# Scores of a threshold attention in tiles of 64 rows by 64 columns, two heads by two halves of 128 queries

## The chip, the cores and the metric

The kernel runs on one core of one Trainium2 chip. Its time is the device time of that core in microseconds (us). The core has five engines that matter here: TensorE (PE in the profile, with its weight loads shown apart as PEld), VectorE (DVE), ScalarE (ACT), GpSimd (POOL) and the queue that issues the transfers (SP).

## The reference

Everything is in float32. For each of 8 batches and 8 heads there are 576 queries, keys and values of 64 features.

```python
scores = (1 / 8) * q @ k.T                       # 576 x 576 for each head
thresh = max(scores, axis=-1) - tau
scores = where(scores >= thresh, scores, -1e9)
attn = exp(scores - max(scores))
attn = attn / (sum(attn) + 1e-9)
o = attn @ v                                     # (8, 8, 576, 64) -> x: (8, 576, 512)
xn = (x - mean(x)) / sqrt(var(x) + 1e-6) * g_ln
out = x + relu(xn @ w_ch1) @ w_ch2               # 512 -> 2048 -> 512
```

## The kernel before, in words

**Steps.** The work is a row of 72 steps, nine (SLOTS) for each batch. In a batch, steps 0 to 3 take one pair of heads each (hp) and the first 256 queries of both heads; steps 5 to 8 take the same pairs and the next 256 queries. Step 4 (s == HP) takes the last 64 queries of all eight heads. So each step has 512 rows of scores against 576 keys, laid out as four blocks of 128 rows.

**Scores.** `scores` (L376) writes into two rooms of PSUM, `sc[0]` and `sc[1]`, one for each head of the pair, of three banks each. Head h lies on partitions 64h to 64h+63 of q and k, so the two heads use the two halves of PE's rows. A block of 128 queries by 576 keys begins at column 128 of its room and the next follows it, so the blocks cross the banks' bounds; `span` (L369) cuts them there into pieces of 384, 192, 320 and 256 columns. The pieces of the two heads are issued in turn. In an ordinary step a product takes 128 queries as its stationary operand (a tile of 64 rows by 128 columns of PE); in step 4 two pairs of heads lie beside each other in each block, so a product takes 64 queries (64 by 64) and `i` goes over two of them. Each product appears in the trace as two instructions of PE.

**After the scores.** `exponentials` (L397) takes the rows' maxima on DVE (neg, L407), the thresholds on POOL (thr, L411) and the exponentials on ACT (e, L419). `weights` (L423) masks, sums (DVE, L426) and divides. The result is turned: in the first batch by products with diagonals on PE (`turn_weights`, tp and tr), later by DVE and a trip through DRAM (`turn_blocks` and `fetch`, which give the tiles em and er).

**Values.** `values_of` multiplies v with the turned weights. The first 512 keys (em, L574) go over all 128 rows of PE and 64 columns, a tile of 128 by 64; the last 64 keys (er, L584) are on 64 rows, a tile of 64 by 64. Except in the first six steps, where both are done at once and er too uses 128 rows (pv in the trace), the er products are put off to the start of the step after next, in the call `run(n, -3)` that stands just ahead of `scores(b, s)` in the main loop (L1007, L1008). The sums lie behind the scores in the same rooms of PSUM (`pv_behind`).

**FFN.** Between the quarters of each step `second_part` (L950) issues pieces of the FFN of groups of 288 tokens: the first product (p) and the second one (seg), which is done as seven products of quarters with sums of quarters of the weights. Every such product goes through `product` (L96), which splits its 128 output rows into two tiles of 128 by 64 that stream the same moving operand.

**Order.** The schedule is written by hand: each engine carries out its instructions in the order in which this program issues them. The queues `later_calls` (by step and quarter), `aside`, `stores` and `drops` say when put-off work is issued. The number of FFN pieces in each quarter follows from counts in the program (ROOM, ends, ready), and not from times.

Of the kernel before, what the change touches and what calls it, by code (L numbers as in the profile page):

```python
# [18 lines left out]
def kernel(  # L19
# [36 lines left out]
    HP = H // 2  # L56
# [307 lines left out]
    sc = [ps_sc.tile([128, 3 * 512], F32, name=f"sc{i}") for i in range(2)]  # L364
# [4 lines left out]
    def span(at, n):  # L369

        while n:
            m = min(n, 512 - at % 512)
            yield at, m
            at, n = at + m, n - m

    def scores(b, s):  # L376


        hp, half = (s, 0) if s < HP else (s - HP - 1, 1)

        pieces = []
        for h in range(2):
            t = 0
            for j in range(2):
                first = FREE + j * S
                for at, n in span(first, S):
                    pieces.append((t, h, j, at, n, at - first))
                    t += n
        for t, h, j, at, n, o in sorted(pieces):
            r = slice(64 * h, 64 * h + 64)  # L390
            for i in range(2 if s == HP else 1):
                qT, kT, ql = turned[b * HP + (2 * j + i if s == HP else hp)]
                nc.tensor.matmul(  # L393
                    sc[h][64 * i : 64 * i + 64 if s == HP else 128, at : at + n],
                    lhsT=ql[r] if s == HP else qT[r, half, j * 128 : (j + 1) * 128],
                    rhs=kT[r, o : o + n], start=True, stop=True,
                )  # L397

# [600 lines left out]
    for n in range(NS):  # L999
        b, s = divmod(n, SLOTS)  # L1000
# [5 lines left out]

        run(n, -3)  # L1007
        scores(b, s)  # L1008
        run(n, -2)
        run(n, -1)  # L1010
# [104 lines left out]
```

## Time and profile before

| | |
|---|---|
| Time, median of 3 runs | 1398.31 us (1396.4 to 1398.57) |
| Span of the profiled execution | 1398.0 us |
| PE matmul busy | 1332.8 us, 95% |
| PE weight load busy | 1011.1 us, 72% |
| DVE, ACT, POOL busy | 928.2, 464.2, 607.1 us |
| Scores of ordinary steps, L393, tile 64*128 | 1024 matmuls, 152.7 us busy |
| Scores of step 4, L393, tile 64*64 | 256 matmuls, median 402 ns |
| Products with v over the first 512 keys, L574, tile 128*64 | 2368 matmuls, 129.5 us busy |
| er products behind, L584, tile 64*64 | 480 of 295 ns and 112 of 230 ns |

Busy times of PE add instructions that run side by side in different tiles only once, and the mean of one is its own length, ends modelled; so a row's count times its mean is more than its busy time. A form such as 64*128 64x384 means a tile of 64 rows and 128 columns, and a moving operand of 64 partitions by 384 elements. In a row of the waits the columns are: who waited, for whom, total us, times, longest us.

### The profile page before, as it was taken

What the parts mean: (1) busy time and instruction counts of PE and PEld (TensorE: products, weight loads), DVE (VectorE), ACT (ScalarE), POOL (GpSimd) and SP (SyncE); (2) the same over time, 40 slices, a digit from 0 to 9 for tenths busy, and PEclk for the clock granted to TensorE, in tenths of its full rate; (3) what the DMA queues carried; (4) which work ended last, traced back from release to release, by engine and by line L of the source; (5) the groups of instructions that cost most, each with busy time, mean ns of one, the idle gap of its engine ahead of it and who ended that gap; (6) DMA issues with size and microseconds to landing.
All of it is one profiled execution on the core that took longest, in us unless ns stands there. A gap on an engine that the chain in (4) does not pass through costs nothing.

```text
span 1398.0 us, 38357 instructions
## 1 busy us (share of the span) xinstructions
PE 1332.8 (95%) x16336; PEld 1011.1 (72%) x16336; DVE 928.2 (66%) x1638; ACT 464.2 (33%) x1003; POOL 607.1 (43%) x807
## 2 busy tenths in 40 slices
PE   4788989999999999999999999999999999999996
PEld 3665655867768696877869687786968687686966
DVE  5898867676776767657776667657675767766211
ACT  3777613232332323232232322323232323323120
POOL 2344444544443544443444445353444444434313
PEclk9999999999999999999999999999999999999998
DMA  9722355446734476446754476445763476343211
GB/s 222 188 77 71 92 139 153 166 141 183 200 128 163 141 196 174 146 141 183 199 159 146 150 191 179 152 150 144 197 181 131 143 183 183 131 162 129 65 18 18
DMA packets 322011, 206.72 MB, mean 148 GB/s; under 512 B 247984, under 2 KB 279472, under 8 KB 313776
## 3 DMA queue, kind: packets, MB, share of 16 engines
q1 hardware_dynamic: 317072, 203.68, 50.2%
q8 instruction: 128, 2.10, 0.6%
q10 hardware_dynamic: 4736, 0.59, 0.4%
q14 instruction: 43, 0.35, 0.1%
q0 software_dynamic: 32, 0.00, 0.0%
HBM read 120.46 MB, written 83.76 MB: 146 GB/s over the span
## 4 chain that ended last, share of the span: by engine, by line
PE 83%; DVE 7%; ACT 2%; DMA 2%; issue 2%; POOL 1%; SPq 1%; POOLq 0%; DVEq 0%; ACTq 0%
PE p L101 34%; PE seg L101 27%; PE sc L393 10%; PE sc L574 8%; PE sc L584 2%; DVE e L426 2%; DVE neg L407 1%; DMA v_in<-in_v_dram 1%; SPq L116 1%; PE tp L101 1%; DMA et<-in_moe_w_ch_dram 1%; POOL q_in L341 1%; PE var L101 0%; PE mean L101 0%; POOL sum L626 0%
## 5 line engine op out<-in xcount | busy, mean ns | idle before, releaser
L101 PE MATMUL p<-xc,w 128*64 128x288 f32 x4096 | 518.1, 408 | 12.9 <-ACT hidden L779 5.5
L101 PEld LDWEIGHTS p<-xc,w 128*64 128x64 f32 x4096 | 287.5, 137 | 219.7 <-ACT hidden L779 16.1
L407 DVE TENSOR_REDUCE neg<-sc 128x2 f32<-128x1152 f32 x144 | 188.7, 1351 | 251.1 <-PE sc L393 251.1
L101 PE MATMUL seg<-hidden,w 128*64 128x144 f32 x3840 | 248.3, 287 | 3.8 <-DVE hidden L847 3.8
L101 PEld LDWEIGHTS seg<-hidden,w 128*64 128x64 f32 x3840 | 234.9, 137 | 14.6 <-issue 6.5
L411 POOL TENSOR_SCALAR thr<-neg,low_sb 128x2 f32<-128x2 f32 x144 | 42.5, 295 | 466.0 <-DVE neg L407 461.0
L442 POOL TENSOR_SCALAR e<-e,den 128x576 f32<-128x576 f32 x252 | 194.3, 785 | 114.5 <-DVE den L431 114.5
L426 DVE SCALAR_TENSOR_TENSOR e<-sc,thr,e 128x576 f32<-128x576 f32 x288 | 221.9, 809 | 16.5 <-POOL thr L411 14.6
L779 ACT ACTIVATE hidden<-p 128x288 f32<-128x288 f32 x256 | 106.6, 417 | 321.9 <-PE p L101 321.8
L419 ACT ACTIVATE e<-sc,neg 128x576 f32<-128x576 f32 x288 | 197.8, 754 | 8.2 <-DVE neg L407 8.2
L393 PE MATMUL sc<-kT,qT 64*128 64x384 f32 (+3 forms) x1024 | 152.7, 429 | 24.1 <-DVE e L426 14.0
L516 DVE STREAM_TRANSPOSE et<-e 128x1152 f32<-128x1152 f32 x112 | 153.2, 1374 | 18.2 <-POOL e L442 17.7
L393 PEld LDWEIGHTS sc<-kT,qT 64*128 64x128 f32 x1024 | 95.6, 192 | 65.3 <-DVE e L426 18.9
L574 PE MATMUL sc<-em,v_in 128*64 128x128 f32 (+1 forms) x2368 | 129.5, 263 | 0.0
L574 PEld LDWEIGHTS sc<-em,v_in 128*64 128x64 f32 x2368 | 122.9, 137 | 7.8
L101 PE MATMUL seg<-hidden,stage 128*64 128x144 f32 x1920 | 123.3, 286 | 0.0
L101 PEld LDWEIGHTS seg<-hidden,stage 128*64 128x64 f32 x1920 | 117.6, 137 | 2.5 <-issue 2.5
L597 ACT COPY x<-sc 128x128 f32<-128x128 f32 x120 | 31.8, 266 | 260.7 <-PE sc L393 193.5
L847 POOL TENSOR_TENSOR hidden<-hidden 128x576 f32<-128x576 f32 x60 | 84.8, 1429 | 47.8 <-ACT hidden L779 38.2
L862 ACT COPY part<-seg 128x288 f32<-128x288 f32 x75 | 30.3, 403 | 198.3 <-PE seg L101 194.2
L847 DVE TENSOR_TENSOR hidden<-hidden 128x576 f32<-128x576 f32 x60 | 49.2, 854 | 49.1 <-PE seg L101 39.1
L101 PE MATMUL seg<-hidden,e 128*64 128x144 f32 x960 | 65.3, 286 | 0.0
(152 smaller groups left out, 1112.9 us busy)
## 6 DMA issues: line engine op xcount, KB each, us to landing
scr<-et SPq DMA_DIRECT2D x63, 1152.0 KB, 5.0
em<-scr SPq DMA_DIRECT2D x63, 1024.0 KB, 5.7
out_dram<-ot SPq DMA_DIRECT2D x256, 36.0 KB, 3.6
q_in<-in_q_dram SPq DMA_DIRECT2D x124, 72.0 KB, 2.5
k_in<-in_k_dram SPq DMA_DIRECT2D x120, 72.0 KB, 2.8
er<-scr SPq DMA_DIRECT2D x126, 64.0 KB, 5.1
v_in<-in_v_dram SPq DMA_DIRECT2D x28, 256.0 KB, 5.5
w<-in_moe_w_ch_dram SPq DMA_DIRECT2D x10, 512.0 KB, 6.2
```

The lines of the kernel that those rows point to most:

```text
L101: nc.tensor.matmul(out[r], lhsT=lhsT[:, r], rhs=rhs, **flags)
L393: nc.tensor.matmul(sc[h][64 * i : 64 * i + 64 if s == HP else 128, at : at + n], lhsT=ql[r] if s == HP else qT[r, half, j * 128 : (j + 1) ...
L407: nc.vector.tensor_reduce(out=neg[:, i], in_=pairs[h], axis=AXL.X, op=ALU.max, negate=True,)
L411: nc.gpsimd.tensor_scalar(out=thr[:, i], in0=neg[:, i], scalar1=-1.0, scalar2=low_sb, op0=ALU.mult, op1=ALU.add,)
L419: nc.scalar.activation(es[:, i], blocks[i], func=AF.Exp, bias=neg[:, i : i + 1])
L426: nc.vector.scalar_tensor_tensor(out=es[:, i], in0=blocks[i], scalar=thr[:, i : i + 1], in1=es[:, i], op0=ALU.is_ge, op1=ALU.mult, accum_o ...
L442: nc.gpsimd.tensor_scalar(out=es[:, i], in0=es[:, i], scalar1=den[:, i : i + 1], scalar2=1.0, op0=ALU.mult, op1=ALU.mult,)
L516: nc.vector.transpose(et[:, :, 64 * h : 64 * h + 64].rearrange("p n (j c) -> p j n c", j=2), es[:, 2 * h : 2 * h + 2].rearrange("p j (n c) ...
L574: nc.tensor.matmul(dst[64 * h : 64 * h + 64], lhsT=vt[:, h, c, :], rhs=pick(em[:, 2 * j : 2 * j + 2, c], h), start=c == 0 and first, stop= ...
L597: nc.scalar.copy(x_of(2 * b + (s > HP))[:, s % (HP + 1), 128 * j : 128 * j + 128], pv[j])
L779: nc.scalar.activation(hidden[:, d], p1, func=AF.Relu)
L847: eng.tensor_tensor(out=out[at], in0=in0[at], in1=in1[at], op=op)
```

## The change

All scores are done in tiles of 64 rows by 64 columns. Where one product took 128 queries, two now take 64 each, written to the lower and upper half of the same 128 partitions. What each computes, the pieces, the streamed columns of kT and the order of the pieces stay as they were. The aim is that the scores use the tiling of PE that the er products with v just ahead of them use, and that four tiles (two heads by two halves) work at once.

```diff
         for t, h, j, at, n, o in sorted(pieces):
             r = slice(64 * h, 64 * h + 64)
-            for i in range(2 if s == HP else 1):
+            for i in range(2):
                 qT, kT, ql = turned[b * HP + (2 * j + i if s == HP else hp)]
                 nc.tensor.matmul(
-                    sc[h][64 * i : 64 * i + 64 if s == HP else 128, at : at + n],
-                    lhsT=ql[r] if s == HP else qT[r, half, j * 128 : (j + 1) * 128],
+                    sc[h][64 * i : 64 * i + 64, at : at + n],
+                    lhsT=ql[r] if s == HP else qT[r, half, j * 128 + 64 * i : j * 128 + 64 * i + 64],
                     rhs=kT[r, o : o + n], start=True, stop=True,
                 )
```

## The prediction

> **What bounds the kernel now.** I read three views in this order: the table of busy time by stretches of 100 us, to see where TensorE (PE) is the limit; the waits of the matmul queue outside the start-up; and the timeline of PE around two blocks of scores, because the kernel before already holds both forms side by side.
>
> ```profile
> 300.00:400.00 100.00, 99.33 (x1135) 72.83 (x1134) 74.30 (x135) 32.17 (x70) 46.09 (x62) 1.00 0.62 172
> ...
> 1100.00:1200.00 100.00, 99.33 (x1138) 72.84 (x1136) 71.10 (x129) 31.77 (x69) 49.13 (x65) 1.00 0.60 170
> ```
>
> The columns are the stretch, its length, then busy us and instructions of PE, weight load (PEld), VectorE (DVE), ScalarE (ACT) and GpSimd (POOL), the granted clock, DMA share and GB/s. From 300 to 1300 us every stretch shows PE busy 98.8 to 99.4 us of 100 at full clock, while DVE, ACT and POOL stay at or below 75 (PEld belongs to PE). Only the first 250 us or so and the last 80 are otherwise. Busy matmuls alone don't prove that PE is at its peak, so I also read what PE waits for from 150 to 1280 us:
>
> ```profile
> PE p L101 <- ACT part L862: 4.0, 7, 0.6
> PE seg L101 <- DVE hidden L847: 3.8, 6, 0.6
> PE p L101 <- ACT hidden L779: 1.8, 1, 1.8
> ```
>
> These are the three largest of nine. All nine come to 14 us, and none of them lies ahead of a score or in the er products. So PE in its written order is what sets the time there, and each tenth of a microsecond saved inside its stream moves the end, as long as the work behind it doesn't turn into a wait.
>
> Now the two blocks of scores, batch 4, some 18 us apart. In the rows: start, length, instructions in the run; after the operation's names comes the shape of the PE tile, rows*columns.
>
> ```profile
> 705.50 2.11 PE L101 MATMUL p<-xc,w 128*64 128x288 f32 x16
> 707.53 0.45 PE L584 MATMUL sc<-er,v_rest 64*64 64x128 f32 x8
> 707.91 2.21 PE L393 MATMUL sc<-kT,qT 64*128 64x384 f32 x16
> 710.05 6.04 PE L101 MATMUL p<-xc,w 128*64 128x288 f32 x48
> ...
> 723.25 3.08 PE L101 MATMUL p<-xc,w 128*64 128x288 f32 x24
> 726.26 0.45 PE L584 MATMUL sc<-er,v_rest 64*64 64x128 f32 x8
> 726.53 2.12 PE L393 MATMUL sc<-kT,q_last 64*64 64x384 f32 x32
> 728.58 4.10 PE L101 MATMUL p<-xc,w 128*64 128x288 f32 x32
> ```
>
> The first is an ordinary step: products of the FFN in tiles of 128*64, the er products in 64*64, the scores in 64*128, the FFN again in 128*64. The second is the step of the last queries (s == HP), whose scores are already in 64*64. Both compute the same number of scores over the same 1152 columns per tile. Ends are modelled, so I take starts only: er to FFN is 710.05 - 707.53 = 2.52 us in the first, 728.58 - 726.26 = 2.32 us in the second. The first loses 0.11 between er and the scores (0.38 against 0.27 from start to start) and 0.09 from the scores to the FFN (2.14 against 2.05).
>
> **What the Trainium skill says.** "TensorEngine Tiling (Array Packing)", Key Properties: "Changing tiling mode (not just tile) drains the TensorE". The trace agrees in kind: with the mode kept from er to scores, the scores start 0.11 us sooner. The same page, Available Configurations, gives four independent tiles for 64x64 and two for 64x128, so both forms can fill the whole array. The trace agrees: 32 instructions of 64*64 take no longer than 16 of 64*128. "TensorE: Matmul & The Clock Gate", LDWEIGHTS, says that the load's time goes with the number of weight columns; here a load takes 187 ns for 128 columns and 133 ns for 64, so the fall is less than half. The tiling page's Gotcha 1 forbids different row tiles to use one PSUM bank at once; the two heads (row tiles) write sc0 and sc1, and that stays.
>
> **The change part by part.** 72 calls of scores() are made, 8 of them in the s == HP form that isn't touched. In the other 64, each of 8 products (16 instructions) of 128 queries becomes two of 64, 16 products (32 instructions), over the same kT columns.
>
> 1. Entrance. Where the er products lie directly ahead, 64*64 is kept instead of switched. I went through all 72 blocks: from the eighth on (120.92 us) the er products always lie directly ahead, in 58 blocks of the changed form and 7 of the other. Start to start is 0.37 to 0.40 us in the 58 and 0.26 to 0.27 in the 7: 0.11 us saved for each.
>
> 2. Streaming. FFN products of 288 columns run x48 in 715.93 - 710.05 = 5.88 us, which is 245 ns for a pair of column tiles. A score tile streams 1152 columns twice, 2304/288 x 245 ns = 1.96 us. The 64*64 block takes 2.05 to the next start and the 64*128 block 2.13 to 2.15 in all 58. So four tiles do run side by side at the full rate, and what is left above streaming shrinks from 0.18 to 0.09: another 0.09 us saved. Why the exit is shorter, fewer weight columns to put in place or a cheaper switch, the trace doesn't say; I need only the sum.
>
> 3. Added instructions. 64 x 16 = 1024 matmuls and as many loads. In a block, PEld goes from 16 x 187 = 3.0 us to 32 x 133 = 4.3 us of load time, but on four tiles at once. The s == HP block carries precisely this count in 2.05 us, so I put it at nothing beyond item 2, hidden beneath the streaming of the other tiles. One thing differs from that block: its two column tiles of one head stream different kT, and the changed block's two stream the same kT. The FFN products do that too: product() at L101 sends one rhs to both column tiles, at the 245 ns a pair used above. Bound: nothing to, if the second tile had to wait for the first, 2 us.
>
> 4. What follows. No wait is added and the order of all other work is kept. The maxima (DVE neg L407) wait on the scores' end and come 0.2 us sooner against the step's start; POOL thr, q_in, DVE qT and once per batch the hidden sum at L847 hang on them, and PE's 0.6 us wait on L847 starts its chain at a score's end, so it moves along unshortened. The wait on ACT part L862 is PE to ACT to PE and keeps its size too. DVE at 63 to 74 of 100 us has room for a step that is about 1.2% shorter. The weights fetched for the values (em<-scr, 5.7 us to land) are asked for at quarter 0 and used at quarter 3 of a step of 17 to 20 us; PE never waits for them now.
>
> Sum: per block 2.52 - 2.32 = 0.20 us. From 246 us on, 52 blocks x 0.20 = 10.4 us, all on the path. The six blocks from 120.92 to 228.34 us lie where the chain of waits runs partly through DVE's and ACT's conversion of weights; of their maxima some three start off PE and the others off a busy DVE, so I count half: 0.6 us. The six changed blocks before 100 us come after 128*64 products (pv), so the entrance switch stays, and PE waits there for DVE anyway: 0 (bound 6 x 0.09 = 0.5). Total 11.0 us: 1398.3 - 11.0 = 1387.3 us.
>
> **Rivals.**
> A. Only the entrance is saved: the exit keeps its 2.14 us because it hangs on something that the s == HP block doesn't have. For it: that block is always followed by FFN products, never by seg. Against: 64*128 blocks leave at 2.14 whether p or seg follows. 58 x 0.11 = 6.4 us, giving 1391.9 us.
> B. The time is taken back by waits: PE reaches ACT's copies or the conversion sooner and stands. For it: start-up shows it. Against: nine kinds of wait at 14 us in all, with DVE at 70%. If less than half came through, 3 to 5 us faster, 1394; at the utmost nothing, 1398.
> C. Slower: shared kT, or the doubled loads, keep the four tiles from running together. If merely the added 16 loads of 133 ns were a tenth exposed, that is 0.2 us x 64 = 14 us, with the switch saved some 3 us slower, 1401; if the two column tiles ran one after the other, 64 x 2 = 128 us, 1526. For it: the exact form isn't in the trace. Against: items 2 and 3.
>
> **How the numbers follow.** Forecast 0.82, A 0.08, B 0.06 (half of it within 0.2%), C 0.04 (a quarter of it within). The range: the low end takes all 58 blocks at 0.20 and the early 0.5 (12.1 us, 1386.2) and below it the spread of the three times before (2.2 us), 1384.3; the high end is just short of A, 1391.5. Outside it is left A, B and C, 0.18. Faster by over 0.2% (2.8 us) 0.93, within it 0.04, slower 0.03.
>
> **What would show it.** Right: L393 in one form only, 64*64 x2304; er to scores 0.27 us and scores to the next product 2.05 us in all blocks after 120 us; PE still busy over 99% from 300 to 1300 us, and its waits at about 14 us. Wrong at item 1: 0.38 stays. Wrong at item 2 or 3: over 2.1 us from scores to the next product, or gaps inside the block. Wrong at item 4: new PE waits on ACT hidden L779, DVE xc L649 or DVE hidden L847, with blocks as short as forecast. Wrong altogether if the span doesn't fall by about 58 times what a block falls.

## The result and the profile after

The changed kernel takes 1388.68 us (median of 4 runs, 1387.83 to 1388.95), the one before, measured beside it, 1397.68 us (4 runs, 1396.4 to 1398.57). The ratio is 0.9935 with a 95% interval of 0.9918 to 0.9952: 9.0 us, and by the interval 7 to 11, against 11.0 forecast. The two profiled executions have spans (first to last instruction) of 1398.0 and 1387.2 us, 10.8 apart. These two overstate the gain a little: their device times are 1399.81 us, above all four runs of the kernel before, and 1388.95.

The timeline of PE of the changed kernel at the block that stood at 707.91 us before. Columns: start, length, engine, line, operation, names, tile and moving operand, count.

```profile
700.48 2.11 PE L101 MATMUL p<-xc,w 128*64 128x288 f32 x16
702.52 0.45 PE L584 MATMUL sc<-er,v_rest 64*64 64x128 f32 x8
702.79 2.12 PE L393 MATMUL sc<-kT,qT 64*64 64x384 f32 x32
704.84 1.43 PE L101 MATMUL p<-xc,w 128*64 128x288 f32 x10
```

The scores now run as 32 instructions in 64*64. From er to the next FFN product it takes 704.84 - 702.52 = 2.32 us, as in the block of step 4 before, and 0.20 less than the 2.52 of the old form. Taken over the 52 changed blocks from 260 us on, the median from er to the next product is 2.520 us before and 2.319 after; the 7 blocks of step 4 keep 2.319. So 52 x 0.201 = 10.4 us. The block at 246 us starts 0.4 us earlier in this trace than in the one before, and that makes the 10.8 us of the spans.

The stretches of 100 us and PE's largest waits from 150 to 1280 us, after:

```profile
300.00:400.00 100.00, 99.32 (x1242) 72.81 (x1240) 75.48 (x139) 31.84 (x69) 45.28 (x61) 1.00 0.63 176
...
1100.00:1200.00 100.00, 99.33 (x1260) 72.77 (x1260) 72.58 (x134) 29.27 (x64) 44.51 (x59) 1.00 0.62 178
```

```profile
PE p L101 <- ACT part L862: 4.0, 7, 0.6
PE seg L101 <- DVE hidden L847: 3.8, 6, 0.6
PE p L101 <- ACT hidden L779: 2.0, 1, 2.0
```

PE is as full as before, with more instructions in each stretch, and its waits have hardly moved: 4.0, 3.8 and 2.0 us where they were 4.0, 3.8 and 1.8. From 250 to 1280 us only the first two are left in either trace, with the same totals. So no wait took the gain back there.

**Where in the block the 0.20 us lay.** Before, I read it as 0.11 ahead of the scores and 0.09 at their end. The starts of single instructions say something else. The numbers are medians over the same 52 blocks, in us. First row: from the first er product to the first score product; second: between the first two passes over the first 384 columns (start to start, the same tile); third: from the start of the last score product to the next FFN product.

```
                                       before, 64*128   after, 64*64
first er product -> first score             0.379           0.269
first pass -> second pass, 384 columns      0.427           0.323
last score product -> next product          0.306           0.306
```

(A pass is the set of instructions that go over one piece of columns, one for each tile at work; each product needs two passes.) From the last product on, both take the same time. In the old form the second pass came 0.10 us late, and both parts of the saving lie at the entrance. Together they are 0.214 us; 0.013 of that goes back because the last of four instructions of a pass starts 0.020 us behind the first, and the last of two 0.007. The weight loads show where the 0.11 and the 0.10 us come from:

```profile
707.53 0.21 PEld L584 LDWEIGHTS sc<-er,v_rest 64*64 64x64 f32 x8 [0.44 <-issue]
707.91 1.81 PEld L393 LDWEIGHTS sc<-kT,qT 64*128 64x128 f32 x16 [0.17 <-issue]
```

```profile
702.52 0.21 PEld L584 LDWEIGHTS sc<-er,v_rest 64*64 64x64 f32 x8 [0.44 <-issue]
702.68 0.26 PEld L393 LDWEIGHTS sc<-kT,qT 64*64 64x64 f32 x8
```

The first pair is the kernel before, the second the one after; the bracket is idle time of the load path ahead of the group. Before, no load of the scores began until 707.91, the moment that is recorded for the first score product itself. After, the first one begins at 702.68, beneath the second pass of the er products, and the scores start at 702.79 without a gap behind that pass.

### The profile page after: what moved, and what is told of

Its sections match the earlier page's. It is cut to its first block, busy times and chain, and to the rows that moved or that the text cites. A ratio compares the mean times of both kernels' runs of the same rounds, so it can differ in the third digit from the quotient of the medians.

```text
span 1387.2 us, 40405 instructions
## 1 busy us (share of the span) xinstructions
PE 1321.1 (95%) x17360; PEld 991.1 (71%) x17360; DVE 927.9 (67%) x1638; ACT 463.3 (33%) x1003; POOL 606.1 (44%) x807
## 4 chain that ended last, share of the span: by engine, by line
PE 82%; DVE 7%; DMA 3%; issue 2%; ACT 2%; SPq 2%; POOL 2%; POOLq 0%; DVEq 0%; ACTq 0%
PE p L101 35%; PE seg L101 27%; PE sc L393 9%; PE sc L574 8%; PE sc L584 2%; DVE e L426 2%; DVE neg L407 1%; SPq L116 1%; DMA v_in<-in_v_dram 1%; PE tp L101 1%; POOL q_in L341 1%; DVE w L272 1%; POOL sum L626 1%; PE var L101 0%; PE mean L101 0%
## 5 line engine op out<-in xcount | busy, mean ns | idle before, releaser
L393 PE MATMUL sc<-kT,qT 64*64 64x384 f32 (+3 forms) x2048 | 147.1, 416 | 22.6 <-DVE e L426 12.6
L393 PEld LDWEIGHTS sc<-kT,qT 64*64 64x64 f32 x2048 | 78.8, 137 | 68.3 <-issue 23.5
```

The costliest lines, as they stand in the source:

```text
L393: nc.tensor.matmul(sc[h][64 * i : 64 * i + 64, at : at + n], lhsT=ql[r] if s == HP else qT[r, half, j * 128 + 64 * i : j * 128 + 64 * i + 64],
```

## The experiments

**Half of the steps.** 64*64 in steps 0 to 3, 64*128 in steps 5 to 8:

```diff
-            for i in range(2):
+            for i in range(2 if s <= HP else 1):
...
-                    sc[h][64 * i : 64 * i + 64, at : at + n],
+                    sc[h][64 * i : 64 * i + 64 if s <= HP else 128, at : at + n],
-                    lhsT=ql[r] if s == HP else qT[r, half, j * 128 + 64 * i : j * 128 + 64 * i + 64],
+                    lhsT=ql[r] if s == HP else qT[r, half, j * 128 + 64 * i : j * 128 + 64 * i + (64 if s < HP else 128)],
```

> 64*64 scores in steps 0 to 3 of each batch alone, 64*128 in steps 5 to 8. If every block gives its 0.20 us for itself (additive), the blocks of batches 2 to 7 give 24 x 0.20 = 4.8 us, those of batch 1 part of 0.8: about 5.2 us under the kernel before, 1392.5 us. If the gain needs all blocks changed, or is set by something other than the blocks: not near half, so nearer 1397 or 1388.

Measured: 1395.29 us beside 1399.24 for the kernel before, ratio 0.9974 (0.9965 to 0.9984), so 3.6 us less by the ratio, with 2.2 to 4.9 inside the interval; the profiled span is 1393.0, 5.0 under the 1398.0 of the kernel before. The two forms stand side by side in one trace:

```profile
705.17 0.45 PE L584 MATMUL sc<-er,v_rest 64*64 64x128 f32 x8
705.44 2.12 PE L393 MATMUL sc<-kT,qT 64*64 64x384 f32 x32
707.49 6.04 PE L101 MATMUL p<-xc,w 128*64 128x288 f32 x48
...
739.14 0.45 PE L584 MATMUL sc<-er,v_rest 64*64 64x128 f32 x8
739.52 2.21 PE L393 MATMUL sc<-kT,qT 64*128 64x384 f32 x16
741.66 0.71 PE L101 MATMUL seg<-hidden,w 128*64 128x144 f32 x8
```

2.32 us for the first, 2.52 for the second, and so in all 24 and 28 of them from 260 us on. By the traces, each block gives its 0.20 us for itself: 24 blocks make 4.8, and the block at 246 us starts 0.15 earlier. The times alone put the gain below the 5.2 expected, which lies just outside their interval; the 4.8 lies just inside.

**The er products in 128*64**, so that neither form of scores meets its own tiling ahead of it. Both kernels get

```diff
-                rows = slice(0, 128) if at_once else slice(64 * j, 64 * j + 64)
+                rows = slice(0, 128)
```

> Scores as in the kernel before (64*128), the er products in tiles of 128*64 like everything ahead of them (zeros of v on the other 64 rows, so the sums are the same, with two tiles at once and not four). The er products then stream 0.22 us more and the switch into them falls away (0.14 us by the gaps in the trace); the switch ahead of the scores stays. Some 58 x 0.08 and, in the 7 blocks of step 4, which gain a switch, 7 x 0.2: 6 us over the kernel before, 1404 us. If a switch costs nothing: 0.22 x 65 = 14 us over, 1412.

> Scores in 64*64 as in the changed kernel, but the er products ahead of them in 128*64, so the switch stays ahead of the scores. Theory 1, all of the 0.20 us is the switch ahead of the scores (a drain, and a first weight load that nothing hides): next to the run with er in 128*64 and scores in 64*128 only the first load gets shorter, 187 to 133 ns, 0.05 us x 55 = 3 us less, 1401 us. Theory 2, as the prediction split it, 0.11 ahead of the scores and 0.09 at their end: 0.09 x 55 = 5 us less, 1399, and from the last score to the next product it takes 0.09 us less than with 64*128. Theory 3, four tiles are simply faster and the switch is nothing: 0.20 x 55 = 11 us less, 1393.

Measured: 1405.76 us with scores in 64*128 (ratio to the kernel before 1.0048, 1.0035 to 1.0062) and 1402.55 with scores in 64*64 (1.0023, 1.0013 to 1.0033). They are 3.2 us apart, what theory 1 asks for and far from the 11 of theory 3; between theories 1 and 2 the trace has to decide.

```profile
712.10 0.61 PE L584 MATMUL sc<-er,v_rest 128*64 128x128 f32 x8
712.64 2.21 PE L393 MATMUL sc<-kT,qT 64*128 64x384 f32 x16
714.78 6.04 PE L101 MATMUL p<-xc,w 128*64 128x288 f32 x48
```

```profile
709.44 0.61 PE L584 MATMUL sc<-er,v_rest 128*64 128x128 f32 x8
709.98 2.17 PE L393 MATMUL sc<-kT,qT 64*64 64x384 f32 x32
712.08 1.19 PE L101 MATMUL p<-xc,w 128*64 128x288 f32 x8
```

With a switch ahead of it the 64*64 block takes 2.10 us to the next product, not 2.05; with 64*128 it is 2.14. From er to the scores both take 0.537 us, and the last product to the next one 0.306 in both. So without the equal tiling ahead of them, four tiles keep only 0.04 us of the 0.20. It is the first pass that is shorter, 0.374 us against 0.427, as the load of 64 columns is against that of 128. That is 52 x 0.041 = 2.1 us; 1.7 of the 3.8 us between these two spans arose before 250 us. Theory 2 is out: with the entrance made equal, no 0.09 us was left at the end.

**Every block of scores twice**, in the kernel before and in the changed one:

```diff
-        for t, h, j, at, n, o in sorted(pieces):
+        for t, h, j, at, n, o in sorted(pieces) * 2:
```

> The kernel before with each block of scores computed twice over, one after the other (64*128; the second writes the same values): the streaming by itself, with one entrance and one exit. All theories: by the distances of its products in the trace 1.94 us more a block, about 130 us of 72 x 1.94 on the path, 1528 us.

> The changed kernel with each block of scores computed twice over (64*64). Theory 1 (all of the gain is at the entrance): again 1.94 us more a block, so as far under the 64*128 double as the changed kernel under the one before, 9 to 11 us, 1518 us. Theory 3 (weights of 64 columns or four tiles stream quicker): what lies in the stream counts double, 0.09 us x 60 = 5 us more, 1513 us. Double loads that don't hide: above 1520 us.

Measured: 1529.48 us (ratio 1.0936, 1.0919 to 1.0952) and 1519.30 us (1.0864, 1.0845 to 1.0882), 10.2 apart. From the first score product to the next FFN product:

```profile
772.35 4.15 PE L393 MATMUL sc<-kT,qT 64*128 64x384 f32 x32
776.43 6.04 PE L101 MATMUL p<-xc,w 128*64 128x288 f32 x48
```

```profile
768.75 4.06 PE L393 MATMUL sc<-kT,qT 64*64 64x384 f32 x64
772.74 6.04 PE L101 MATMUL p<-xc,w 128*64 128x288 f32 x48
```

In both, a block takes 1.94 us more: 2.141 becomes 4.081 and 2.050 becomes 3.990 (medians). Twice the products, twice the loads, and the same 10 us: nothing of the gain lies in the stream, and the added loads of the 64*64 form are hidden entirely once a block is running.

**One product more between er and the scores**, on a constant tile, into columns of sc0 that nothing reads, from step 7 on. R and C are the rows and columns of its tile.

```diff
         run(n, -3)
+        if n >= SLOTS - 2:
+            nc.tensor.matmul(
+                sc[0][:C, :64], lhsT=avg_sb[:R, :C], rhs=avg_sb[:R, :64],
+                start=True, stop=True,
+            )
         scores(b, s)
```

> The changed kernel with one small product (64 columns, on a constant tile, into unused columns of sc0) between the er products and the scores, in steps 7 to 71; here in 64*64, so without any switch. It is the control for the next three: 2 instructions of 64 columns, between nothing (beside the other three tiles) and 0.11 us (alone): 0 to 7 us over the changed kernel, 1389 to 1396 us.

> The same small product in 128*64: more rows, the same columns, and two switches more in each of 65 steps. Theory 1 (a switch is a drain of 0.09 us and a first load of 0.05 us that nothing hides): 2 x 0.14 us x 60 = 17 us over the control, and from er to the scores 0.28 us more. If only a change of columns makes PE drain: as the control.

> The same small product in 64*128: the same rows, more columns, the switch that the change took away, and one back. Theory 1: (0.195 + 0.14) x 60 = 20 us over the control. If only a change of rows makes PE drain: as the control, and then the 0.11 us of the prediction's entrance were something else.

> The same small product over the whole array: rows and columns change. If the two kinds of change add up, 0.28 + 0.335 us a step: 37 us over the control. If there is one kind of drain whatever changes: as with 64*128, 20 us.

```
tile of the product   time, us   over 64*64   er to next FFN product, us   over 64*64
64*64                 1395.27                  2.416
128*64                1414.51      19.2        2.738                       0.322
64*128                1421.35      26.1        2.842                       0.426
128*128               1422.51      27.2        2.845                       0.429
```

These are single runs of each, so the reading rests on the distances in the trace, medians of 52 steps. Two switches cost 0.32 us where all loads have 64 columns, so one costs 0.16: 0.11 ahead of the first product, and 0.05 in its first pass. From er to the product put in it takes 0.379 us in 128*64, in 64*128 and in 128*128 alike, and 0.269 in 64*64. A change of rows alone makes PE stop, a change of columns alone too, and the two don't add up: both at once cost no more than columns alone. One kind of drain would give this. Here is the third:

```profile
717.63 0.45 PE L584 MATMUL sc<-er,v_rest 64*64 64x128 f32 x8
718.01 0.43 PE L1009 MATMUL sc<-avg_sb 64*128 64x64 f32 x2
718.37 2.17 PE L393 MATMUL sc<-kT,qT 64*64 64x384 f32 x32
720.47 0.71 PE L101 MATMUL p<-xc,w 128*64 128x288 f32 x4
```

0.38 us from er to the product in 64*128 is what the kernel before paid ahead of its scores, and the scores behind it, now 64*64, take 2.10 us to the next product, as every 64*64 block with a switch ahead does. I had expected 20 us over the control and 26 came. The two passes of the product are 0.16 us apart, and 0.11 in 128*64; from the second pass to the scores it takes 0.20 us, and 0.15 in 128*64. Both fit a load of 128 columns that a product so short can't hide, in the second pass as in the first; for the second this is not shown. For 128*64 I had expected 0.28 us more from er to the scores. It is 0.36, of which 0.04 comes back behind: in the control the product streams beside the scores. So the distance to the FFN is the fair one.

**The halves apart.** All products of the lower 64 queries first, then the upper ones:

```diff
-        for t, h, j, at, n, o in sorted(pieces):
-            r = slice(64 * h, 64 * h + 64)
-            for i in range(2):
+        for i in range(2):
+            for t, h, j, at, n, o in sorted(pieces):
+                r = slice(64 * h, 64 * h + 64)
```

The rest of the call stays as it was.

> 64*64 scores, but all products of the lower 64 queries first and then all of the upper ones (step 4 likewise, by its two pairs). If tiles run at once only where their products are neighbours in the order of issue, two of four tiles work at a time: 1.94 us more for each of 72 blocks, about 130 us of it on the path, near 1519 us. If PE looks far enough ahead to bring the halves together, or streams of one half are as quick: 1389 us.

Measured: 1457.90 us, one run: 69 us over the changed kernel, between the two expectations. A block takes 3.08 us to the next product where it took 2.05, so two of four tiles work alone for 1.03 us and not for 1.94.

```profile
718.76 0.45 PE L584 MATMUL sc<-er,v_rest 64*64 64x128 f32 x8
719.03 3.15 PE L393 MATMUL sc<-kT,qT 64*64 64x384 f32 x32
722.11 11.86 PE L101 MATMUL p<-xc,w 128*64 128x288 f32 x96
```

The single starts show the upper half's first two instructions at 720.02 us, ahead of six of the lower half that stand before them in the program (starting at 720.27 to 720.77). The columns tell them apart: the two have 384, and all four of the lower half with 384 had started by 719.37; the six have 320 and 256. So PE does run tiles past each other, but only so far. That four tiles work at once in the changed kernel rests on `i` being the innermost loop.

## Why the prediction was right, and where not

**The bound.** Right. PE's order set the time from 250 us on, and every 0.20 us inside it arrived at the end: 52 blocks make 10.4 of the 10.8 us between the spans. The 10.4 lies within the 7 to 11 of the timed runs.

**Item 1, the entrance.** Right in size and mechanism: 0.379 became 0.269 us. The product in 64*128 between er and the scores brought back the 0.38, and the er products in 128*64 took the advantage away. The Trainium skill, "TensorEngine Tiling (Array Packing)", Key Properties, says that a change of tiling mode drains TensorE. The traces agree, in that neither a load nor a product of the new tiling begins at once, and put it at 0.11 us here.

**Item 2, streaming and exit.** The size was right (2.141 to 2.050 us), the place wrong. I took starts from one group to the next, and "exit" was only what was left over; the last product to the next one takes 0.306 us in every form. The 0.09 us is the first pass: after a switch, the first weights weren't loaded beneath the products ahead, and the second pass of the first piece comes late, 0.427 against 0.323 us in 64*128, where that load is recorded with 183 ns. In 64*64 with a switch ahead it is 0.374 us and 129 ns: the first pass and the load grow by the same 0.05 us. The sum held because I took er to FFN as one distance, measured on a block that had the new form already.

**Item 3, the added instructions.** Right: nothing beyond item 2. The doubled blocks add 1.94 us in both forms, and shared kT runs as quickly as different kT (2.319 us in both kinds of step).

**Item 4, what follows.** Right: no new wait on PE from 250 us on. The start-up stays open: 0.6 us forecast, 0.4 by the two traces. In the other pairs of traces the block at 246 us moved by more than the change can give, 1.7 us one way with er in 128*64 and 1.1 the other way with doubled blocks, so 0.4 is within what the start-up varies by.

**The rivals.** A rested on an exit that differs between the two forms, and it doesn't. B's waits didn't grow. C's worst end, column tiles one after the other, can be had by the order of issue alone, and even then costs 69 us and not 128, since PE reaches some products ahead.

The time, 1388.7, is 1.4 us above the 1387.3 forecast, and the 9.0 us of gain 2.0 under the 11.0; the unchanged kernel's runs scattered by as much (1396.4 to 1398.6), so no cause can be given for the gap. (The profiled span of 1387.2 is no closer hit: the device time of that execution was 1388.95.) The low end of the range has a slip: 1386.2 less 2.2 is 1384.0, not 1384.3.

## What to carry to other kernels

Where PE is full, look for places where its tile changes shape, and measure from the start of a group ahead to the start of a group behind: here a change costs 0.16 us with a first load of 64 columns and 0.20 with one of 128, however few products follow. Give a short group the tile shape of its neighbour, even with twice the instructions, if the halves are neighbours in the order of issue. If a kernel has one step that already uses the new form, that step is a good estimate of the change: here it took 2.319 us from er to the FFN, and so do the changed blocks, though the first account of where the 0.20 us lay was wrong.

## What the runs showed of the hardware that was not expected

- A switch costs more than the 0.11 us ahead of the first product. The first weight load behind it isn't hidden, and the first pass is longer by 0.05 us with 64 columns (0.374 against 0.323) and by 0.10 with 128 (0.427).
- Instructions for idle tiles start ahead of earlier ones for busy tiles: with the halves apart, two of the upper half started at least 0.25 us before six that the program has ahead of them.
- A change of both the rows and the columns of the tile costs no more than one of the columns: 0.429 and 0.426 us for 128*128 and 64*128, each there and back. The wait ahead of the first product is the same for rows, columns or both.
